# A decode step on one core: another plan of heads, and new orders of every engine's work

## The chip, the core and the metric

The kernel runs on one core of one Trainium2 chip. The core has five engines, each with its own instruction stream: TensorE (PE, with its weight loads shown as PEld), VectorE (DVE), ScalarE (ACT), GpSimd (POOL) and SyncE (SP), which here only issues transfers. The metric is the device time of one execution in microseconds (us): the median of the runs of a kernel. The span is the time from the first to the last instruction in the profile.

## The reference

Four sequences (B = 4), one new token each, model width 448. There are two layers with the same weights, each an attention block and an FFN block, with a layer norm ahead of each and a residual add behind:

```python
W = min(4096, max(256, Sk // 4))                  # 2048 of 8192 cached keys
q = (x @ wq).reshape(B, Sq, Hq, Dh)               # 16 query heads, 8 K/V heads, Dh = 256
k = jnp.repeat(k_cache[:, :, Sk - W:, :], rep, axis=1)
v = jnp.repeat(v_cache[:, :, Sk - W:, :], rep, axis=1)
scores = jnp.einsum("bhqd,bhkd->bhqk", q, k) * (Dh ** -0.5)
p = _softmax(scores, axis=-1)
o = jnp.einsum("bhqk,bhkd->bhqd", p, v)           # then o @ wo
x = x + _A_ref(_layernorm(x), ...)                # attention
x = x + _B_ref(_layernorm(x), ...)                # FFN: (silu(x @ w_gate) * (x @ w_up)) @ w_down
# ... and both once more
```

Each (sequence, K/V head) has a window of K and one of V, 1 MB each in bf16; 32 such pairs are needed in each layer. Both layers read the same 64 MB of cache. The weights are about 12 MB.

## The kernel before

**Heads and groups.** A head is named by three digits, sequence, layer and K/V head: 215 is sequence 2, layer 1, head 5. `PLAN` lists the heads in steps; a step's heads joined with `+` or `&` form one softmax group of two heads, and a group with `&` computes its scores head by head. A group runs through: scores (L878, PE), maximum (L894, DVE), two matmuls that spread it (L899, L902), its negative (L908), exp (L912, ACT), a turn of the probabilities (L925, PE) and their copy (L934, ACT), sums (L942, L947), P.V in two halves of a V matrix for each head (L956, PE), the pick of the right parts (L971 ACT, L973 DVE), a flip (L979, PE), the scaling into `oT` (L989, DVE) and the output projection, as rows (L1009) or, at a sequence's last step of a layer, as columns (L1001).

**Between layers.** When a sequence has all eight heads of a layer, its rows are folded in (L746, L748, L756), the residual is added (L764), and the norm runs (L519, L522 on DVE, L525 and L533 on PE, three small operations on POOL). Behind layer 0 follow its FFN, as columns (gate and up L705, down L733) for sequences 0 and 3 or as rows (L641, L669) for 1 and 2, and the projection of its queries for layer 1 (L579, L595, L610). Sequences that have ended layer 1 wait and share an FFN with a later one. The last FFN serves sequences 2 and 3 and ends the kernel.

**Memory.** K and V live in a pool of 27 slots of half a matrix (512 KB). `KEEP_K` and `KEEP_V` say how many heads of each sequence keep K or V from layer 0 to layer 1, so that they are loaded once. K has to be transposed by DVE in place, half by half (L845, 1232 ns each). The heads in `WHOLE` load K in one 1-MB transfer (L833), the others in two (L839); V always comes in two (L855). All transfers are issued by SyncE in one order. A load into a used slot waits for the last reader of what lay there, and whatever stands behind it in SyncE's order waits too.

**Orders.** `SEQ_PE`, `SEQ_DVE`, `SEQ_ACT`, `SEQ_POOL` and `SEQ_SP` list every operation of each engine in its order, by number; `SLOTS` gives each load its slot. An engine never runs ahead of its list. `w6` in `SEQ_PE` is a filler: a matmul of 128x512 on zeros into bank A (L1084) whose result adds nothing. It stands behind the 6th operation of another engine on bank A, and the 7th waits for it:

```python
if x[0] == "w":
    o, k = Op(len(self.ops), PE, "fw", filler), max(int(x[1:]), 1)
    o.deps[inA[max(k, 1) - 1]] = True
    if k < len(inA):
        inA[k].deps[o] = True
```

`DUR` holds a duration for each kind of operation. The order doesn't come from it: it only decides which waits are already covered by others and need not be written.

Of the kernel before, what the change touches and what calls it, by code (L numbers as in the profile page):

```python
# [35 lines left out]
KEEP_K = (6, 5, 4, 7)  # L36
KEEP_V = (5, 5, 4, 4)
ROWF = (1, 2)
PLAN = (
# [4 lines left out]
)  # L44
WHOLE = (
    "000 001 104 111 112 205 207 312 315 317"
)
SEQ_PE = (
# [32 lines left out]
)  # L81
SEQ_DVE = (
# [67 lines left out]
    guc1=.51, tanhc=.27, downc=1.65, rowcp=.54, rturn=.35, orow=.53, xin=.26, tr=1.24, qe=.29, sc1=.85, sc2=1.5, sch=1.2, max1=.25,  # L150
# [1000 lines left out]
```

## Time and profile before

| | |
|---|---|
| runs | 294.18, 295.67, 296.25 us; median 295.67 |
| profiled execution | 294.49 us, its span 292.6 us |
| mean granted TensorE clock | 0.953 |
| busy PE, PEld, DVE, ACT, POOL | 251.8, 137.6, 187.3, 63.2, 84.4 us |
| bytes loaded | 104.45 MB, mean 359 GB/s |
| fillers (L1084) | 294, 86.0 us busy |

A row of a time line gives the start, the length, the engine, the line and the operation, `out<-in` by the program's names, the shape and the count; in brackets stands idle time ahead of it and what ended it. `half` is the pool of K and V, `S`, `Y`, `Z` and `A` are banks of PSUM. SPq is SyncE's queue of DMA issues; a row that merges issues lasts from the first to the last of them, waits included. Matmuls overlap, so that their rows can be longer than what they add. A busy PE says little here, because fillers keep it busy while it waits.

### The profile page before, as it was taken

To read this page: it belongs to the slowest core of one execution; us is meant where nothing else is said; L and a number is where in the kernel's file an instruction comes from. 1 tells how busy PE (TensorE), PEld (TensorE's weight loads), DVE (VectorE), ACT (ScalarE), POOL (GpSimd) and SP (SyncE) were. 2 spreads that over 40 slices of the span, in tenths; PEclk is the share of its full clock that TensorE was granted. 3 is DMA by queue.
4 is the path that set the end of the run, shared out by engine and by line. 5 is a ranking of instruction groups with operands and counts; after the bars stand their busy time and mean duration, and the time that the engine had idled before them with its cause. 6 is when DMAs were issued, how large, how long until landed. Compare 5 with 4: busy or idle time off the path is not lost.

```text
span 292.6 us, 10922 instructions
## 1 busy us (share of the span) xinstructions
PE 251.8 (86%) x4814; PEld 137.6 (47%) x4814; DVE 187.3 (64%) x581; ACT 63.2 (22%) x176; POOL 84.4 (29%) x225
## 2 busy tenths in 40 slices
PE   0689889998999797988989978898798999799886
PEld 0334433334564463444435644544445447565554
DVE  8514985677114497658767969877596786336732
ACT  0030211212003121211333312313223221122310
POOL 1530231211304142403132453322444312244150
PEclk9999999999899797999999979999999995999959
DMA  7999999999999999989999999999999998599500
GB/s 266 401 392 407 410 410 407 408 408 404 391 407 325 381 393 406 408 317 313 413 405 395 417 414 407 407 409 409 403 374 410 409 398 270 212 330 399 230 4 3
DMA packets 29903, 105.15 MB, mean 359 GB/s; under 512 B 2968, under 2 KB 7072, under 8 KB 28448
## 3 DMA queue, kind: packets, MB, share of 16 engines
q1 hardware_dynamic: 29856, 104.45, 91.6%
q8 instruction: 38, 0.62, 0.9%
q14 instruction: 9, 0.07, 0.1%
HBM read 104.44 MB, written 0.00 MB: 357 GB/s over the span
## 4 chain that ended last, share of the span: by engine, by line
PE 44%; DMA 25%; DVE 18%; issue 5%; SPq 4%; ACT 2%; POOL 1%; DVEq 0%; ACTq 0%
DMA half<-in_A_k_cache_dram 15%; PE A L1084 11%; DMA half<-in_A_v_cache_dram 10%; DVE half L845 9%; PE Y L956 8%; PE S L878 8%; PE Z L705 3%; PE A L1009 2%; SPq L839 2%; DVE oh L973 2%; PE Z L733 2%; PE Z L525 2%; SPq L855 1%; DVE tiny L894 1%; PE S L899 1%
## 5 line engine op out<-in xcount | busy, mean ns | idle before, releaser
L845 DVE STREAM_TRANSPOSE half<-half 128x1024 uint32<-128x1024 uint32 x84 | 102.8, 1232 | 10.6 <-DMA half<-in_A_k_cache_dram 10.3
L1084 PE MATMUL A<-identb,small 128*128 128x512 bf16 x294 | 86.0, 394 | 0.7 <-ACT wide L746 0.5
L969 POOL TENSOR_TENSOR small<-small 128x2 f32<-128x2 f32 (+1 forms) x49 | 39.0, 797 | 67.2 <-DVE small L947 65.9
L956 PE MATMUL Y<-half,pT 128*4 128x256 bf16 (+1 forms) x1024 | 48.6, 283 | 9.2 <-issue 4.0
L878 PE MATMUL S<-half,qe 128*8 128x128 bf16 (+1 forms) x1568 | 46.0, 239 | 4.9 <-issue 2.6
L878 PEld LDWEIGHTS S<-half,qe 128*8 128x8 bf16 x1568 | 30.8, 85 | 17.0 <-DVE half L845 6.6
L884 POOL TENSOR_TENSOR qe<-qc,tiny 128x64 bf16<-128x64 bf16 x64 | 18.2, 293 | 70.6 <-PE S L878 57.6
L1084 PEld LDWEIGHTS A<-identb,small 128*128 128x128 bf16 x294 | 25.4, 101 | 20.0 <-issue 4.1
L912 ACT ACTIVATE praw<-S,small 104x128 bf16<-104x128 f32 (+1 forms) x49 | 19.6, 399 | 59.7 <-DVE small L908 59.5
L956 PEld LDWEIGHTS Y<-half,pT 128*4 128x4 bf16 (+1 forms) x1024 | 20.5, 85 | 23.7 <-DMA half<-in_A_v_cache_dram 8.4
L971 ACT ACTIVATE oh<-Y 128x256 bf16<-128x256 f32 x49 | 18.7, 383 | 53.1 <-PE Y L956 46.7
L973 DVE SCALAR_TENSOR_TENSOR oh<-oh,small,Y 128x256 bf16<-128x256 bf16 x49 | 23.1, 471 | 9.5 <-ACT oh L971 9.1
L894 DVE TENSOR_REDUCE tiny<-S 104x1 bf16<-104x128 f32 (+1 forms) x49 | 15.8, 324 | 17.6 <-PE S L878 17.0
L934 ACT ACTIVATE pT<-Y 128x64 bf16<-128x64 f32 (+1 forms) x49 | 12.5, 256 | 46.7 <-PE Y L956 26.3
L1009 PE MATMUL A<-wo_sb,oT 128*4 128x448 bf16 x188 | 17.3, 365 | 0.1
L541 POOL TENSOR_SCALAR st<-st 128x1 f32<-128x1 f32 x16 | 4.2, 265 | 34.5 <-DVE st L531 32.2
L947 DVE TENSOR_REDUCE small<-Y 128x2 f32<-128x32 f32 (+1 forms) x49 | 9.4, 192 | 7.4 <-PE Y L942 7.0
L525 PE MATMUL Z<-st,small 128*128 128x2 f32 x32 | 7.3, 299 | 7.5 <-DVE st L522 7.1
L989 DVE TENSOR_TENSOR oT<-Y,small 128x4 bf16<-128x4 f32 (+1 forms) x63 | 8.4, 151 | 7.7 <-PE Y L979 4.1
L899 PE MATMUL S<-small,identb 104*104 104x32 bf16 x49 | 10.6, 218 | 2.6 <-DVE tiny L894 1.7
L908 DVE TENSOR_REDUCE small<-S 104x1 f32<-104x32 f32 x49 | 8.7, 180 | 6.2 <-PE S L902 3.9
L899 PEld LDWEIGHTS S<-small,identb 104*104 104x104 bf16 x49 | 6.1, 126 | 11.9 <-DVE tiny L894 8.8
(132 smaller groups left out, 255.3 us busy)
## 6 DMA issues: line engine op xcount, KB each, us to landing
half<-in_A_v_cache_dram SPq DMA_DIRECT2D x92, 512.0 KB, 9.7
half<-in_A_k_cache_dram SPq DMA_DIRECT2D x68, 512.0 KB, 9.7
half<-in_A_k_cache_dram SPq DMA_DIRECT2D x8, 1024.0 KB, 9.7
wo_sb<-in_A_wo_dram SPq DMA_DIRECT2D x8, 448.0 KB, 11.4
wq_sb<-in_A_wq_dram SPq DMA_DIRECT2D x3, 1024.0 KB, 6.8
wd_sb<-in_B_w_down_dram SPq DMA_DIRECT2D x1, 1568.0 KB, 16.7
wg_sb<-in_B_w_gate_dram SPq DMA_DIRECT2D x1, 1344.0 KB, 13.1
wu_sb<-in_B_w_up_dram SPq DMA_DIRECT2D x1, 1344.0 KB, 15.2
```

Of the source, the lines that this page charges most:

```text
L845: return e.transpose(a, a)
L878: last = e.matmul(Sb[s_][qd:qd + 8, 0:32 * 2 * J], lhsT=qe[q_][:, P, ce, :, :].rearrange("p a n -> p (a n)"), rhs=keys(kcs[P], J * x, J, c ...
L884: g.op(POOL, "qe", lambda e, P=P, t=t, kvh=kvh: e.tensor_tensor(qe[q_][:, P, :, :, :], qc[t][:, kvh, :, :].unsqueeze(2).broadcast_to([128, ...
L894: g.op(DVE, f"max{n}", lambda e: e.tensor_reduce(pmax[s_][0:R, :], Sb[s_][0:R, 0:N], AX.X, ALU.max), r=(f"s{s_}",), w=(f"pmax{s_}",), bank ...
L899: e.matmul(Sb[s_][0:R, 256:288], lhsT=identb[0:R, 0:R], rhs=far[0:R, :, :, :].broadcast_to([R, 2, 8, 2]) if n == 2 else far1[0:R, :, :].br ...
L912: return e.activation(praw[0:R, 0:128 * n].rearrange("p (g r l) -> p g r l", g=2 * n, l=2), Sb[s_][0:R, 0:128 * n].rearrange("p (l g r) -> ...
L956: last = e.matmul(Yb[p_][32 * gg:32 * gg + M, 256:512], lhsT=pT[pt][:, gg, 2 * a + hv, 4 * P:4 * P + M] if n == 2 else p1[:, gg % 2, 2 * a ...
L969: g.op(POOL, f"pow{n}", lambda e: e.tensor_tensor(ri[p_][:, 0:2 * n], rs[p_][:, 0:2 * n], expo[:, 1:1 + 2 * n], op=ALU.pow), r=(f"rs{p_}", ...
L971: g.op(SCA, "oh", lambda e: e.activation(oh[:, :], Yb[p_][:, 256:512], ACT.Copy), r=(f"y{p_}",), w=("oh",), bank=(f"Y{p_}",))
L973: g.op(DVE, "oho", lambda e: e.scalar_tensor_tensor(out=oh[:, :], in0=oh[:, :], scalar=lomask[:, 0:1], in1=Yb[p_][:, 256:512], op0=ALU.mul ...
L1009: last = e.matmul(Ab[32 * k:32 * k + B, 0:D], lhsT=oT[oi][:, k % 2, k // 2, :], rhs=wo_sb[:, 4 * kvh + k, :], start=False, stop=False, ski ...
L1084: return e.matmul(Ab[:, 0:512], lhsT=zero[:, 0:1].broadcast_to([128, 128]), rhs=identb[:, :].unsqueeze(1).broadcast_to([128, 4, 128]), sta ...
```

## The change

Only tables change. `PLAN` has 50 groups (36 of one head, 14 of two) instead of 49 (34 and 15), in another order. 39 matrices are kept instead of 40: K 21 for 22, V 18 as before, but shared out otherwise. `WHOLE` names 18 heads instead of 10; of these, 15 instead of 8 are really loaded, since the others keep K from layer 0. So SyncE issues 182 transfers instead of 187. All five orders and the slots are new, the fillers are 344 instead of 294, and two durations in `DUR` differ. The text of the kernel is one line longer, so that from `SEQ_PE` on its line numbers are one higher.

```diff
-KEEP_K = (6, 5, 4, 7)
-KEEP_V = (5, 5, 4, 4)
+KEEP_K = (5, 5, 4, 7)
+KEEP_V = (6, 5, 4, 3)
 PLAN = (
-    "000 001", "004 006", "005", "002 003", "007", "101", "100", "102", "014", "013", "016&015", "017+107", "106",
-    "105", "104+103", "012 201+202 011", "204", "010 117+200", "114 113", "115&206", "203", "116", "207+205",
-    "112&111", "110", "302&303", "300 215", "213", "304+216", "307", "306", "301&217", "305", "212", "210",
-    "214 316+314", "311&315", "317+310", "313+211", "312",
+    "000", "002 005", "004", "007", "006", "001", "003", "102", "100", "101", "013", "016", "011+104",
+    "015+014 105", "017", "106+103", "107", "201 010", "200", "202", "012", "204&116", "110+203", "114", "115",
+    "207", "206", "113+205", "112+302", "117&306", "305", "111 213", "217+300", "307", "304+216", "303 301", "215",
+    "212", "210 214", "313+317", "311+314", "211", "312+315", "316&310",
 )
 WHOLE = (
-    "000 001 104 111 112 205 207 312 315 317"
+    "000 002 003 004 005 006 007 010 011 100 101 102 107 114 115 200 202 206"
 )
 SEQ_PE = (
-    "51 55 58 65 68 w1 75 w1 78 w1 85 w1 88 97 98 100 101 103 w1 w1 104 w1 106 w1 w1 w1 w1 w1 w1 w1 w1 w1 w1 w1 "
+    "w1 w1 w1 w1 w1 51 55 w1 w1 w1 58 w1 w1 65 w1 w1 w1 68 w1 w1 w1 w1 75 w1 w1 w1 w1 78 w1 w1 w1 85 w1 w1 97 w1 "
...
 SEQ_SP = (
-    "46 47 48 49 50 162 163 212 213 239 287 288 314 117 140 166 168 189 191 120 121 216 218 143 144 241 243 170 "
+    "50 46 47 142 48 49 117 120 190 121 214 164 238 146 264 193 145 262 139 242 287 361 167 217 168 186 212 236 "
...
-    guc1=.51, tanhc=.27, ... max1=.25,
+    guc1=.6, tanhc=.27, ... max1=.29,
```

The rows below are of the built programs, PE's instructions in their order, without times. `half` with `pT` is P.V, `half` with `qe` scores, `A<-identb,small` a filler, `wg_sb` and `wu_sb` gate and up, `wd_sb` down, `wo_sb` the output projection, `st,small` the norm's sums.

PE before, around the first row fold of sequence 1 (L756), while the V of heads 104 and 103 is used:

```order
L1084 MATMUL A<-identb,small 128x512 x2
L956 MATMUL Y<-half,pT 8x256 x8
L756 MATMUL Z<-tiny,wide 128x1 x8
L956 MATMUL Y<-half,pT 8x256 x8
L1084 MATMUL A<-identb,small 128x512 x13
L956 MATMUL Y<-half,pT 8x256 x8
L878 MATMUL S<-half,qe 8x256 x32
L956 MATMUL Y<-half,pT 8x256 x8
```

PE after, around the same fold (there L757):

```order
L1085 MATMUL A<-identb,small 128x512
L757 MATMUL Z<-tiny,wide 128x1 x8
L943 MATMUL Y<-pT,tiny 128x32
L980 MATMUL Y<-tiny,oh 128x2 x2
L1085 MATMUL A<-identb,small 128x512
L957 MATMUL Y<-half,pT 4x256 x8
L1085 MATMUL A<-identb,small 128x512
L926 MATMUL Y<-sel,praw 64x32 x4
L957 MATMUL Y<-half,pT 4x256 x8
```

Before, 13 fillers stand in a row between two P.V halves; after, fillers stand singly between the groups' operations.

PE before, in the FFN behind sequence 3's layer 0 (`wg_sb` to `wd_sb`):

```order
L956 MATMUL Y<-half,pT 4x256 x8
L533 MATMUL Z<-xn,twice 128x1
L705 MATMUL Z<-xn,wg_sb 128x32 x42
L705 MATMUL Z<-st,wg_sb 128x32 x14
L705 MATMUL Z<-xn,wu_sb 128x32 x42
L705 MATMUL Z<-st,wu_sb 128x32 x14
L979 MATMUL Y<-tiny,oh 128x2 x2
L1084 MATMUL A<-identb,small 128x512 x2
L733 MATMUL Z<-wide,wd_sb 128x32 x56
L1009 MATMUL A<-wo_sb,oT 4x448 x4
L925 MATMUL Y<-sel,praw 64x32 x4
L878 MATMUL S<-half,qe 8x128 x32
```

PE after, in the same FFN:

```order
L534 MATMUL Z<-xn,twice 128x1
L706 MATMUL Z<-xn,wg_sb 128x32 x42
L706 MATMUL Z<-st,wg_sb 128x32 x14
L926 MATMUL Y<-sel,praw 64x32 x4
L706 MATMUL Z<-xn,wu_sb 128x32 x42
L943 MATMUL Y<-pT,tiny 128x32
L706 MATMUL Z<-st,wu_sb 128x32 x14
L957 MATMUL Y<-half,pT 4x256 x16
L879 MATMUL S<-half,qe 8x128 x32
L926 MATMUL Y<-sel,praw 64x32 x4
L734 MATMUL Z<-wide,wd_sb 128x32 x56
```

The P.V of head 212 moved from ahead of gate and up to behind them, the scores of head 214 (the last row before) from behind the down matmuls to ahead of them, and the two fillers ahead of the down matmuls went.

PE before, from the last P.V to the last FFN:

```order
L956 MATMUL Y<-half,pT 4x256 x16
L533 MATMUL Z<-xn,twice 128x1
L756 MATMUL Z<-tiny,wide 128x1 x8
L1084 MATMUL A<-identb,small 128x512
L979 MATMUL Y<-tiny,oh 128x2 x2
L1084 MATMUL A<-identb,small 128x512
L1001 MATMUL A<-oT,wo_sb 128x1 x16
L1084 MATMUL A<-identb,small 128x512 x2
L525 MATMUL Z<-st,small 128x2
L1084 MATMUL A<-identb,small 128x512
L705 MATMUL Z<-xn,wg_sb 128x32 x42
```

PE after, the same stretch:

```order
L957 MATMUL Y<-half,pT 8x256 x32
L757 MATMUL Z<-tiny,wide 128x1 x8
L1085 MATMUL A<-identb,small 128x512
L980 MATMUL Y<-tiny,oh 128x4 x2
L1085 MATMUL A<-identb,small 128x512
L1002 MATMUL A<-oT,wo_sb 128x1 x32
L534 MATMUL Z<-xn,twice 128x1
L526 MATMUL Z<-st,small 128x2
L1085 MATMUL A<-identb,small 128x512
L534 MATMUL Z<-xn,twice 128x1
L706 MATMUL Z<-xn,wg_sb 128x32 x42
```

The last group now has two heads (316 and 310, before 312 alone), so that two column projections stand there, and the two fillers behind them went.

More of the change, by code (lines that the diff above doesn't have):

```diff
@@ L149 @@
     qturn=.25, qsel=.28, rvh=.24, rvt=.28, gur3=1.2, gur1=.7, tanhr=.69, fturn=.26, downr=.93, fh=.23, ft=.29, guc3=1.26,
-    guc1=.51, tanhc=.27, downc=1.65, rowcp=.54, rturn=.35, orow=.53, xin=.26, tr=1.24, qe=.29, sc1=.85, sc2=1.5, sch=1.2, max1=.25,
+    guc1=.6, tanhc=.27, downc=1.65, rowcp=.54, rturn=.35, orow=.53, xin=.26, tr=1.24, qe=.29, sc1=.85, sc2=1.5, sch=1.2, max1=.29,
     max2=.42, spread=.3, negm=.18, exp1=.36, exp2=.47, turn1=.26, turn2=.35, pt1=.22, pt2=.33, tot1=.19, tot2=.23,
```

165 rows, old and new, of tables (SEQ_ACT, SEQ_DVE, SEQ_PE, SEQ_POOL) are left out of this document.

## The prediction

> **What bounds the kernel now.** The page comes first: what it moves, and what the chain that ended last is made of.
>
> ```profile
> span 292.6 us, 10922 instructions
> PE 44%; DMA 25%; DVE 18%; issue 5%; SPq 4%; ACT 2%; POOL 1%; DVEq 0%; ACTq 0%
> q1 hardware_dynamic: 29856, 104.45, 91.6%
> ```
>
> The chain is PE's for 44% and a transfer's for 25%. These are averages over stages with different limits, so the second view is busy time by stretch, cut where the transfer rate changes (columns: PE, PEld, DVE, ACT, POOL busy; granted clock; DMA share; GB/s).
>
> ```profile
> 0.00:90.00 90.00, 74.73 (x1075) 35.81 (x1079) 49.62 (x179) 11.95 (x36) 19.96 (x58) 0.98 1.00 391
> 90.00:126.00 36.00, 30.74 (x637) 16.26 (x629) 24.02 (x60) 9.49 (x27) 11.46 (x28) 0.91 1.01 387
> 126.00:157.00 31.00, 27.98 (x541) 14.00 (x537) 21.95 (x61) 7.55 (x19) 8.41 (x25) 1.00 0.95 361
> 157.00:239.00 82.00, 71.90 (x1535) 41.00 (x1523) 64.80 (x179) 22.74 (x63) 28.64 (x74) 0.98 1.02 406
> 239.00:277.00 38.00, 34.52 (x821) 22.61 (x819) 21.85 (x76) 9.61 (x27) 11.93 (x30) 0.91 0.82 302
> 277.00:292.60 15.60, 11.96 (x250) 7.91 (x246) 5.01 (x30) 1.88 (x6) 3.99 (x11) 0.78 0.01 3
> ```
>
> Take 406 GB/s, the rate over the longest full stretch, as what the loads get when nothing holds them back. Each stretch then lost (1 - rate/406) of its length: 3.3, 1.7, 3.4, 0, and 9.7 us from 239 to 277. After that 15.6 us have no loads at all. So transfers set the pace up to 239 us. From there PE does, and the loads wait for it.
>
> The third view is the SyncE queue and PE around the two stretches that lose, first 126 to 157.
>
> ```profile
> half<-in_A_v_cache_dram SPq DMA_DIRECT2D x1, 512.0 KB, 15.3
> 111.18 5.59 SPq L855 DMA_DIRECT2D half<-in_A_v_cache_dram  x2
> 116.82 13.84 SPq L839 DMA_DIRECT2D half<-in_A_k_cache_dram  x4
> 126.07 2.98 PE L1084 MATMUL A<-identb,small 128*128 128x512 bf16 x13
> 128.98 0.39 PE L956 MATMUL Y<-half,pT 128*8 128x256 bf16 x8
> 129.20 1.09 PE L878 MATMUL S<-half,qe 128*8 128x256 bf16 x32
> ```
>
> The first row is the DMA view of 111 to 112 us: that half of V landed 15.3 us after its issue at 111.18, at 126.5. The P.V matmuls on it (L956) began at 128.98, because 13 fillers stood ahead of them. The scores behind (L878) ended at 130.3, and the queue, which needed their slot, had nothing issued before that. Without the run the P.V starts at about 126.5: 2.5 us.
>
> From 239 on, PE's time line reads so:
>
> ```profile
> 237.75 0.39 PE L956 MATMUL Y<-half,pT 128*4 128x256 bf16 x8
> 242.31 1.07 PE L878 MATMUL S<-half,qe 128*8 128x128 bf16 x32
> 247.08 0.60 PE L705 MATMUL Z<-st,wu_sb 128*128 128x32 bf16 x14
> 248.45 1.56 PE L733 MATMUL Z<-wide,wd_sb 128*128 128x32 bf16 x56
> 253.20 0.82 PE L579 MATMUL Z<-wq_sb,xn 128*4 128x512 bf16 x12
> 258.53 2.05 PE L878 MATMUL S<-half,qe 128*8 128x256 bf16 x48
> 278.30 0.61 PE L956 MATMUL Y<-half,pT 128*4 128x256 bf16 x16
> 280.41 0.59 PE L1001 MATMUL A<-oT,wo_sb 128*128 128x1 bf16 x16
> 280.86 1.01 PE L1084 MATMUL A<-identb,small 128*128 128x512 bf16 x2
> 282.54 0.59 PE L525 MATMUL Z<-st,small 128*128 128x2 f32 x2 [0.66 <-DVE st L522]
> ```
>
> At 237.75 the last P.V of sequence 3's layer 0 runs. Its FFN and q projection follow, strictly in PE's order, and only at 258.53 do the first scores of sequence 3's layer 1 start: 20.8 us. Five groups follow, to the last P.V, which ends at 278.9: 20.4 us. The tail to 292.6 is 13.7. The sum is 54.85.
>
> **The change part by part.** *Bytes.* One head matrix fewer is kept: 105.49 MB instead of 104.44, +1.05 MB, or 2.6 us at 406 GB/s if the loads decide the end. If PE's chain after 237.75 decides it, another count matters. By the SyncE order and the sizes on the page, the half of V that ends sequence 3's layer 0 is now the load with which 90.80 MB are in; before it was 91.85. That stretch begins 1.05 MB earlier: **-2.6**. In exchange 14.69 MB instead of 12.59 come behind it.
>
> *1-MB transfers.* Fifteen loads of K instead of eight go in one transfer. The rows give no price to that: 157 to 239 holds both sizes at 406 GB/s, the sizes' common limit, so **0**. What covers it is the queue of issued loads. [...]
>
> *The filler run.* The order now puts single fillers between the operations there: **-2.5**. The row next to it bounds it: between 0 (the queue then waits for the next group) and 3.4, all that the stretch lost.
>
> *Early work.* Fillers go from 294 to 344, and 43 of the 50 added ones stand where the first 30 MB are still coming in and transfers set the pace. By 2.98/13 = 0.23 us each they are 10 us of PE time, hidden behind the queue: by the new order 17 MB are issued before the first load that waits for a slot. **0**. If that cover were gone, it would be up to those 10. Reordered set-up on DVE and K ahead of V at the start are hidden by the same loads.
>
> *Sequence 3's FFN.* Between the marks 237.75 and 258.53 the new order has the same FFN and projection, and in addition the scores of one head (L878, 0.63 us, the price just ahead of the mark, quoted below), a pair of P.V halves (0.61, as at 278.30), a column projection (0.59, as at 280.41), a row projection (0.4, taken like a P.V half) and two fillers (0.23 each): 2.7 us.
>
> ```profile
> 237.29 0.63 PE L878 MATMUL S<-half,qe 128*8 128x128 bf16 x32
> ```
>
> Lower end 0 (PE waited there anyway), upper end 5.4, twice as much, if the transposes it needs come late. I take **+2.7**, since PE is busy 3.8 to 4.0 of 4 us in that stretch (rows below).
>
> *Five last groups.* The same five (four of two heads, one of one), with 1 filler instead of 9: 8 x 0.23 = **-1.8**, between 0 and -3.
>
> *Tail.* The residual add waited for two fillers behind the projection:
>
> ```profile
> 281.91 0.16 DVE L764 TENSOR_TENSOR xr<-xr,A 128x4 f32<-128x4 f32 x1 [1.56 <-PE A L1084]
> ```
>
> The projection ended at 281.0, the add began at 281.9. That 0.9 goes, and a second column projection comes in (L1001, at most 0.59, taken as 0.4 since PE overlaps them): **-0.5**. What is then late is the norm's chain on DVE.
>
> *The rest.* One more softmax group adds small operations to stretches in which PE has work for 74.7 of 90 or 71.9 of 82 us, and the two new numbers in the table of durations change which waits are written out, not the order: **0**.
>
> **Sum**, on the profiled execution: 292.6 - 2.6 - 2.5 + 2.7 - 1.8 - 0.5 = **287.9 us span**. That execution took 294.49, 1.9 over its span, and the median of the runs shown is 295.67, another 1.2: 287.9 + 3.1 = **291.0**, 1.6% less. A difference of 1% (3.0 us) is about what a measurement of this kernel can tell from no change.
>
> **The rivals.** *The loads decide.* If PE keeps ahead, the 14.69 MB after the mark take 36.2 us at 406 GB/s. The mark stands at 237.75 - 5.1 = 232.7, so they end at 268.9, and with a P.V (0.6) and a tail of 13.2 the span is 282.7, the time 285.8. For it: the transposes of the last K now come earlier. Against it: the rate was 302 in this stretch.
>
> *A cold clock.* Where the clock was down, PE was not idle:
>
> ```profile
> 240.00:244.00 4.00, 3.77 (x70) 2.32 (x71) 2.59 (x11) 0.00 (x0) 0.76 (x2) 0.69 0.76 284
> 244.00:248.00 4.00, 4.00 (x126) 3.50 (x119) 2.49 (x8) 0.93 (x3) 1.66 (x5) 0.50 0.90 280
> ```
>
> The same score group took 1.07 us at 242.31, against 0.63 before. Of about 6.5 us below full clock, 41% is lost: 2.7 us. With 1 filler instead of 9 among the last groups such a stretch could fall there: span 290.6, time 293.7. [...]
>
> *The queue runs dry earlier, and it is slower.* The FFN of sequence 2 lies at 190 to 210. The DMA views of 178 to 184 us (first two rows) and of 209 to 214 (last two) show what it ate of the queue's stock:
>
> ```profile
> half<-in_A_v_cache_dram SPq DMA_DIRECT2D x3, 512.0 KB, 13.8
> half<-in_A_k_cache_dram SPq DMA_DIRECT2D x3, 512.0 KB, 13.4
> half<-in_A_k_cache_dram SPq DMA_DIRECT2D x3, 512.0 KB, 8.1
> half<-in_A_v_cache_dram SPq DMA_DIRECT2D x3, 512.0 KB, 7.3
> ```
>
> From issue to landing it fell from 13.6 to 7.7: 5.9 us of stock used, no load held up. Counted through the new order, the loads freed during this FFN stand only 2.1 to 3.2 MB (5 to 8 us) behind the one that their releaser needs; before it was 2.6 to 5.2. If the stock is gone when the FFN starts, these 5.9 us are lost, and with the same at sequence 1 the 2.5 aren't won: 287.9 + 8.4 = 296.3, time 299.4, slower by 1.3%. It decides once the loads lose over 8 us between 126 and 239. Against it: PE has 10 us without work in the 82 of that stretch.
>
> *The gains are given back.* The FFN of sequence 3 costs its upper end (+2.7), and the filler run another wait (+2.5): 293.1, time 296.2, no change.
>
> **How the numbers follow.** Forecast 0.50, the loads decide 0.12, cold clock 0.12, dry queue 0.14, given back 0.12. The forecast's own range is 288.5 to 293.5 by the ends of its small terms; a sixth of it lies above 292.7, where 1% begins. Faster: 0.42 + 0.12 = 0.54. Within 1%: 0.08 + 0.12 of the clock, 0.04 of the dry queue (half its price), 0.08 of the last = 0.32. Slower: 0.10 + 0.04 = 0.14. The range, 285.0 to 298.5, takes in all but most of the dry queue and some of each end.
>
> **What would show it.** In the profile after: no run of over ten fillers ahead of a P.V at about 125 us, and 126 to 157 near 390 GB/s. The mark (last P.V of sequence 3's layer 0) at about 233; the first scores of its layer 1 some 23.5 us later; the last P.V 18.6 after that; a tail near 13.2. The prediction is wrong if the rate between 157 and 230 falls under 390 (the dry queue), or if the last groups' P.V wait for transfers rather than for PE's own order.

## The result, and the profile after

Changed kernel: 287.2 us (median of 4, 285.39 to 291.14), beside 295.89 (4 runs, 294.18 to 296.25); the ratio is 0.970 (0.963 to 0.976). Run once more (e1 below) it gave 288.7 beside 295.35, 0.980 (0.969 to 0.990). Forecast were 291.0 and 1.6% less; it is 2 to 3% less. 287.2 lies inside the whole range (285.0 to 298.5), but below the forecast's own (288.5 to 293.5). Executions over 1.5% above the quickest of their kernel are left out of the ratios and of all medians below, and as both traced executions of the changed kernel (291.1 and 292.9 us) are such, run e3, the same orders in an execution of 288.3, stands beside them where lengths are compared. By that the changed kernel's median over both runs is 287.2 (6 executions).

The page of the changed kernel, the same three lines as before:

```profile
span 289.4 us, 11132 instructions
PE 41%; DMA 37%; DVE 14%; SPq 3%; ACT 2%; issue 2%; POOL 0%; DVEq 0%
q1 hardware_dynamic: 29136, 105.50, 93.6%
```

"issue" went from 5% of the chain to 2%. Busy time by stretch, columns as before (PE, PEld, DVE, ACT, POOL busy; granted clock; DMA share; GB/s):

```profile
0.00:90.00 90.00, 77.14 (x1111) 39.03 (x1111) 48.14 (x178) 11.80 (x36) 18.05 (x55) 1.00 1.00 394
90.00:126.00 36.00, 32.68 (x677) 16.74 (x677) 27.76 (x61) 9.20 (x27) 11.59 (x30) 1.00 1.01 391
126.00:157.00 31.00, 27.45 (x520) 14.32 (x516) 23.90 (x71) 8.55 (x23) 9.74 (x30) 0.94 1.00 389
157.00:239.00 82.00, 70.32 (x1523) 39.42 (x1522) 61.63 (x172) 22.08 (x61) 26.94 (x74) 0.99 1.00 394
239.00:277.00 38.00, 34.70 (x872) 23.27 (x870) 23.32 (x85) 11.26 (x31) 13.47 (x36) 0.93 0.88 324
277.00:289.40 12.40, 8.27 (x222) 6.51 (x222) 3.68 (x24) 0.79 (x3) 3.16 (x10) 0.82 0.01 3
```

From 126 to 157 the loads go from 361 to 389 GB/s, from 239 to 277 from 302 to 324. Then the marks on PE's time line, and the residual add on DVE's:

```profile
235.62 0.39 PE L957 MATMUL Y<-half,pT 128*4 128x256 bf16 x8 [1.48 <-DMA half<-in_A_v_cache_dram]
258.99 2.03 PE L879 MATMUL S<-half,qe 128*8 128x256 bf16 x64 [0.63 <-POOL qe L885]
275.52 1.29 PE L957 MATMUL Y<-half,pT 128*8 128x256 bf16 x32
278.28 0.95 PE L1002 MATMUL A<-oT,wo_sb 128*128 128x1 bf16 x32
```

```profile
279.27 0.16 DVE L765 TENSOR_TENSOR xr<-xr,A 128x4 f32<-128x4 f32 x1 [0.71 <-PE Z L534]
```

The mark (last P.V of sequence 3's layer 0) is at 235.6, 23.4 us later the first layer-1 scores of sequence 3 start, 17.8 later the last P.V ends (276.8), and the tail is 12.55. In e3:

```profile
232.85 0.39 PE L958 MATMUL Y<-half,pT 128*4 128x256 bf16 x8
255.13 1.12 PE L880 MATMUL S<-half,qe 128*8 128x256 bf16 x32 [0.63 <-POOL qe L886]
273.14 0.39 PE L958 MATMUL Y<-half,pT 128*8 128x256 bf16 x8 [0.59 <-DMA half<-in_A_v_cache_dram]
```

So 232.9, then 22.3, 18.4 and a tail of 12.6 (span 286.1). (A variant's line numbers are off by a few.) From the mark to the last P.V it takes 41.2 us before, and 41.2 and 40.7 after. What was won lies ahead of the mark and in the tail.

### The profile page after: what moved, and what is told of

Read it like the earlier page. It is cut to its first block, busy times and chain, and to the rows that moved or that the text cites. A ratio compares the mean times of both kernels' runs of the same rounds, so it can differ in the third digit from the quotient of the medians.

```text
span 289.4 us, 11132 instructions
## 1 busy us (share of the span) xinstructions
PE 250.6 (87%) x4912; PEld 139.3 (48%) x4912; DVE 188.4 (65%) x587; ACT 63.7 (22%) x179; POOL 82.9 (29%) x234
## 4 chain that ended last, share of the span: by engine, by line
PE 41%; DMA 37%; DVE 14%; SPq 3%; ACT 2%; issue 2%; POOL 0%; DVEq 0%
DMA half<-in_A_k_cache_dram 22%; DMA half<-in_A_v_cache_dram 15%; PE A L1085 11%; PE S L879 8%; DVE half L846 8%; PE Y L957 6%; PE Z L706 3%; PE A L1010 2%; PE Y L926 2%; PE Z L734 2%; PE A L1002 1%; DVE oh L974 1%; SPq L834 1%; PE Z L580 1%; SPq L492 1%
## 5 line engine op out<-in xcount | busy, mean ns | idle before, releaser
L846 DVE STREAM_TRANSPOSE half<-half 128x1024 uint32<-128x1024 uint32 x86 | 105.2, 1233 | 12.6 <-DMA half<-in_A_k_cache_dram 12.5
L1085 PE MATMUL A<-identb,small 128*128 128x512 bf16 x344 | 102.4, 395 | 5.2 <-DVE A L420 4.8
L957 PE MATMUL Y<-half,pT 128*4 128x256 bf16 (+1 forms) x1024 | 44.7, 275 | 7.5 <-DMA half<-in_A_v_cache_dram 4.7
L879 PE MATMUL S<-half,qe 128*8 128x128 bf16 (+1 forms) x1600 | 42.6, 238 | 6.1 <-POOL qe L885 2.1
L1085 PEld LDWEIGHTS A<-identb,small 128*128 128x128 bf16 x344 | 29.4, 103 | 31.9 <-issue 9.6
L879 PEld LDWEIGHTS S<-half,qe 128*8 128x8 bf16 x1600 | 29.5, 85 | 18.0 <-POOL qe L885 4.1
L957 PEld LDWEIGHTS Y<-half,pT 128*4 128x4 bf16 (+1 forms) x1024 | 19.0, 83 | 20.4 <-DMA half<-in_A_v_cache_dram 6.7
L935 ACT ACTIVATE pT<-Y 128x64 bf16<-128x64 f32 (+1 forms) x50 | 12.6, 251 | 36.0 <-PE Y L926 31.5
L1037 POOL MEMSET oT<- 128x16 bf16 x40 | 4.1, 111 | 36.8 <-PE A L1010 24.1
L926 PE MATMUL Y<-sel,praw 104*64 104x32 bf16 x144 | 8.8, 193 | 4.0 <-ACT praw L913 3.6
L980 PEld LDWEIGHTS Y<-tiny,oh 128*128 128x128 bf16 x100 | 6.9, 100 | 10.7 <-DVE oh L974 5.4
```

The source lines that it names most:

```text
L846: return e.transpose(a, a)
L879: last = e.matmul(Sb[s_][qd:qd + 8, 0:32 * 2 * J], lhsT=qe[q_][:, P, ce, :, :].rearrange("p a n -> p (a n)"), rhs=keys(kcs[P], J * x, J, c ...
L926: last = e.matmul(Yb[p_][64 * h:64 * h + 64, c0:c0 + (48 if n == 2 else 32)], lhsT=praw[0:R, 64 * gg:64 * gg + 64], rhs=w, start=(gg == 0) ...
L957: last = e.matmul(Yb[p_][32 * gg:32 * gg + M, 256:512], lhsT=pT[pt][:, gg, 2 * a + hv, 4 * P:4 * P + M] if n == 2 else p1[:, gg % 2, 2 * a ...
L1085: return e.matmul(Ab[:, 0:512], lhsT=zero[:, 0:1].broadcast_to([128, 128]), rhs=identb[:, :].unsqueeze(1).broadcast_to([128, 4, 128]), sta ...
```

## The experiments

In the table all lengths are read from PE's time line of the one traced execution; "issue" is the sum of PE's idle pieces of 0.35 us and more, from 90 us on, that the trace puts down to nothing but issue.

```
run                     median (n)   beside  ratio (95%)            mark  to scores  to last P.V  tail   issue
before                  -            -       -                     237.8     20.8         20.4  13.7     6.6
e2  before, no run      292.7 (9)    293.8   0.996 (0.991-1.000)   234.6     18.2         22.8  13.7     6.6
e5  before, end         294.7 (9)    294.9   0.999 (0.994-1.003)   238.6     21.2         20.2  12.9     6.8
e9  before, less bytes  294.6 (9)    293.6   1.006 (1.002-1.010)   236.4     20.9         20.1  13.6     7.0
after                   286.7 (3)    295.9   0.970 (0.963-0.976)   235.6     23.4         17.8  12.6     0.0
e1  after again         288.0 (3)    293.8   0.980 (0.969-0.990)   235.7     23.3         19.6  12.6     0.0
e3  after, split        287.4 (2)    293.8   0.978 (0.968-0.989)   232.9     22.3         18.4  12.6     0.0
e4  after, 43 fewer     287.1 (1)    293.8   -                     230.4     21.5         20.8  12.6     2.1
e6  after, less ahead   287.0 (5)    294.9   0.971 (0.966-0.976)   230.8     23.6         18.3  12.6     2.3
e7  after, less behind  286.1 (5)    294.9   0.969 (0.964-0.974)   229.5     21.9         18.1  12.6     0.7
e8  after, no FFN fill  286.1 (3)    294.9   0.969 (0.963-0.976)   233.0     21.4         20.9  12.9     0.0
e10 after, none early   290.7 (9)    293.6   0.990 (0.987-0.994)   230.6     26.4         20.8  12.6     5.0
e11 after, P.V ahead    286.8 (5)    293.6   0.979 (0.973-0.986)   231.6     21.6         18.9  12.6     0.0
e12 e11 and e8          286.3 (4)    293.6   0.977 (0.971-0.982)   233.3     21.7         21.2  12.6     0.0
```

### e1: the change again

No edit.

> The changed kernel once more, unaltered, for a second trace. Its first traced execution took 291.14 us; its three others took 285.4 to 287.7. In that first trace sequence 3's layer 0 ends (last P.V) at 235.6 us, first layer-1 scores of sequence 3 at 259.0 (23.4 later), the last P.V ends at 276.8 (17.8 later), the tail is 12.6, and the loads ran at 379 GB/s from 190 to 215 us. Theory A (the PE order from that P.V on is a fixed chain of 23.4 + 17.8 + 12.6 us, and only the loads ahead of it vary): a trace with a time near 287 has the P.V at about 231.5, the same three lengths within 0.7 us, and 190 to 215 near 400 GB/s. Rival B (the last stretches vary): the P.V stays at about 235 and the lengths behind it are 4 us shorter.

The trace took 292.9, and its mark was at 235.7 again, so theory A was not put to the test as meant. The later traces do that: executions of 283.8 to 288.3 (e3, e4, e6, e7, e11) have the mark at 229.5 to 232.9. The length from the mark to the last P.V is not fixed, but moves only between 40.7 and 42.9 in the traces that keep the orders and the bytes behind the mark (after, e1, e3, e4, e6), with one exception: 47.2 in e10.

### e2: the run of 13 fillers alone

```diff
-... 603 615 604 w6 w6 w6 w6 w6 w6 w6 w6 w6 w6 w6 w6 w6 605 703 606 705 ...
+... 603 615 604 605 703 606 705 ...
```

> The kernel before without the 13 fillers that stand ahead of the P.V at 128.98 us; nothing else is changed. Forecast's step: 2.5 us sooner, so the last P.V of sequence 3's layer 0 starts at about 235.2 instead of 237.75, 126 to 157 us runs at about 390 GB/s instead of 361, and the time is about 293.2. Rival (the queue then waits for the next group): 361 rises by less than 10, time 295.7, no change.

The stretch 126 to 157 and the marks of e2:

```profile
126.00:157.00 31.00, 29.21 (x584) 15.18 (x576) 22.95 (x66) 8.76 (x23) 9.19 (x27) 0.94 1.01 391
```

```profile
234.55 0.39 PE L956 MATMUL Y<-half,pT 128*4 128x256 bf16 x8
252.77 1.42 PE L878 MATMUL S<-half,qe 128*8 128x256 bf16 x38
275.01 0.61 PE L956 MATMUL Y<-half,pT 128*4 128x256 bf16 x16
```

391 GB/s instead of 361, as forecast; the other two traces of the order before, e5 and e9, have 369 and 355 there. The mark came 3.2 sooner, in one trace beside one. The median is 1.2 lower, with an interval from 0 to 2.6. The place is right; of the size the times say no more than that.

### e5: the fillers of the end alone

```diff
-... 1516 1496 w28 1541 ... 1501 1519 w28 1521 1544 w28 1505 ... 1631 w33 1627 w33 1633 w33 w33 1637 ...
+... 1516 1496 1541 ... 1501 1519 1521 1544 1505 ... 1631 w33 1627 w33 1633 1637 ...
```

> The kernel before, with 8 of the 9 fillers among its five last groups taken out, and the two that stand behind its last column projection. Forecast's steps: from the first layer-1 scores of sequence 3 to the end of the last P.V 18.6 us instead of 20.4, and the tail behind it shorter by the 0.9 that the residual add waited, 12.8 instead of 13.7; the time 2.7 lower than the kernel before beside it. Rival (cold clock): the granted clock over the last groups, 1.00 in the trace of before, falls to about 0.9 and the stretch stays at 20 us. Rival (loads): the last load landed at 276.4 and its P.V can't end ahead of about 277, so of 1.8 at most that much comes; the P.V then waits for a transfer.

```profile
238.60 0.39 PE L955 MATMUL Y<-half,pT 128*4 128x256 bf16 x8
259.77 1.96 PE L877 MATMUL S<-half,qe 128*8 128x256 bf16 x48
279.36 0.61 PE L955 MATMUL Y<-half,pT 128*4 128x256 bf16 x16
```

```profile
282.08 0.16 DVE L763 TENSOR_TENSOR xr<-xr,A 128x4 f32<-128x4 f32 x1 [0.69 <-PE A L1000]
```

Two answers in one trace. The tail fell from 13.71 to 12.87, the 0.9 that the add had waited; now it waits for the projection (L1000). The five groups took 20.2 instead of 20.4: taking eight fillers out of them gave nothing, and the clock there stayed at 1.00, so the cold clock was not what ate it. Nor were the loads: the last one landed at 278.7, 1.3 ahead of the end of the last P.V, and no wait of PE in the five groups is put down to a load. PE's waits there, of 0.15 us and more and all put down to DVE and ACT, went from 0.7 to 2.7 us: where the fillers ran, PE now waits for the groups' own small operations. The tail's gain does not show in the median (0.2 of 294.9, with an interval of -1.8 to 1.0).

### e3: 1-MB transfers split

```diff
-                        g.dma(1 << 20, lambda e, kc=kc, ksrc=ksrc: e.dma_start(
-                            kv[:, HALF * kc[0][0]:HALF * kc[0][0] + 2 * HALF], ksrc[:, :]), None, ...
+                        g.dma(1 << 20, lambda e, kc=kc, ksrc=ksrc: tuple(e.dma_start(
+                            kv[:, HALF * (kc[0][0] + b):HALF * (kc[0][0] + b + 1)], ksrc[:, HALF * b:HALF * (b + 1)])
+                            for b in range(2)), None, ...
```

> The changed kernel with each of its 15 transfers of 1 MB issued as two of 512 KB, one behind the other, on the same place in the queue, into the same slots and behind the same waits. Forecast's step (the size of a transfer is worth 0): 287.2 within 1 us. Rival (1-MB transfers move faster: the first 29 us brought 11.1 MB after and 10.6 before, 1.3 us at 406 GB/s): 288.5 to 289.5, with the loss ahead of 90 us, where 14 of the 15 are. A third, that the smaller pieces land sooner and help: 286.

Its four runs (286.4 to 292.8) don't tell 0 from the rival's 1.3 us. In the trace PE's operations between 75 and 135 us come up to 1.3 us later than in the changed kernel's first trace, and from 155 on level or sooner; beside e6, which has the same orders and the 1-MB transfers, they come 2 to 3 us later from 40 to 97 us. The first 29 us brought 362 GB/s in e3 (366 or 367 in the traces of the order before) and 373 to 389 in the nine other traces of the new orders: 0.3 to 0.8 MB, which is 0.8 to 1.9 us at 406 GB/s. That speaks for the rival, in the place that it names, though e3 has one trace; what it is worth at the end stays open.

### e6 and e9: fewer bytes ahead of the mark

```diff
+                        if (t, layer, kvh) in ((3, 0, 0), (3, 0, 7)):
+                            g.dma(1 << 18, lambda e, cell=cell, hv=hv, vsrc=vsrc: e.dma_start(
+                                unit(cell)[:, 0:HALF // 2], vsrc[hv][:, 0:HALF // 2]), None, ...
```

e6 has this in the changed kernel, e9 in the kernel before, there for heads 2 and 3.

> The changed kernel with 1.05 MB less to load ahead of the end of sequence 3's layer 0: the four V halves of its heads 0 and 7 bring 256 KB each instead of 512 (the second half of each is left out of the computation; the same number of transfers, slots and waits). Forecast's step (the mark moves with the bytes ahead of it, 2.6 us per 1.05 MB at 406 GB/s): last P.V of layer 0 of sequence 3 about 2.6 sooner against the bytes' pace, the loads' queue no longer in the way, and the time 284.5 to 285.5. Rival (PE's order ahead of the mark decides it): time 287 to 288, no change.

> The kernel before with 1.05 MB less to load ahead of the end of sequence 3's layer 0: the four V halves of its heads 2 and 3 bring 256 KB each (their second half is left out of the computation). They land at 201 to 207 us in the trace of before, where a load had 11 to 13 us from issue to landing. Forecast's step (in the kernel before, bytes ahead of the mark set it): the last P.V of sequence 3's layer 0 at about 235.2 instead of 237.75 (238.6 in the other undisturbed trace), time 292.5 beside 295. Rival (as in the changed kernel, where the same cut gave nothing: the issue of the next loads waits for PE's FFN of sequence 2, and the stock is only used up sooner): the mark within 0.8 us of before, the rate from 200 to 230 us under 385, time 294.5 to 295.

The stretch 200 to 230, first e3 and e6, then the kernel before and e9, each from its own windows:

```profile
200.00:230.00 30.00, 26.07 (x638) 15.58 (x639) 23.44 (x71) 8.99 (x24) 9.47 (x29) 1.00 1.02 403
```

```profile
200.00:230.00 30.00, 26.10 (x596) 15.02 (x585) 21.87 (x68) 9.17 (x26) 10.52 (x34) 0.94 0.97 354
```

```profile
200.00:230.00 30.00, 25.79 (x591) 14.61 (x583) 22.18 (x70) 8.89 (x24) 11.27 (x32) 1.00 1.01 400
```

```profile
200.00:230.00 30.00, 26.50 (x628) 15.57 (x626) 22.38 (x71) 9.17 (x25) 11.07 (x32) 1.00 0.99 385
```

In e6 the rate fell by 49 GB/s over 30 us, which is 1.5 MB, and the DMA share from 1.02 to 0.97: the loads behind did not use the room. Each is issued only when its slot is free, and what SyncE waited for between 196 and 226 us was in every case a matmul of PE. The half of V that the mark's P.V reads was issued at 220.74 in e6 and took 10.0 us; in e4 and e7, with all the bytes ahead of the mark, it was issued at 219.94. The time is that of the changed kernel. In e9 the mark of the one trace came 1.4 sooner, but its runs were 0.6% slower than before, not 0.9% faster. A megabyte ahead of the mark is not worth 2.6 us in either kernel. That step of the forecast fell.

### e7: fewer bytes behind the mark

The same edit for heads 0 and 4 of sequence 2's layer 1.

> The changed kernel with 1.05 MB less to load behind that mark: the four V halves of heads 0 and 4 of sequence 2's layer 1 bring 256 KB each (their second half is left out of the computation). Forecast's step (behind the mark PE's chain decides, the number of bytes there doesn't): time within 0.7 us of the changed kernel, the last load lands about 2 us sooner and the last P.V does not. Rival (the loads decide the end): 2 to 2.6 us sooner, with the last P.V moving together with the last load. By the traces so far it lies between: in two of them the last P.V ended 0.7 to 1.0 us behind the last landing, in another 2.9 behind.

286.1, 1.1 under the changed kernel's 287.2, and 0.9 under e6, whose bytes were cut to no use; neither is clear of the spread. Mark to last P.V took 40.0, and the last P.V ended 0.75 behind the last landing (268.7). The number of bytes behind the mark is worth less than the rival's 2 to 2.6, and may be worth nothing.

### e8, e11 and e12: the stretch behind the mark

e8 takes out the 12 fillers there, e11 moves two P.V halves (1417, 1418) ahead, e12 does both:

```diff
-... 1342 1415 1343 w27 1351 w27 1347 w27 1417 1353 w27 1354 1418 1211 1433 w28 w28 1422 ...
+... 1342 1415 1417 1418 1343 1351 1347 1353 1354 1211 1433 1422 ...
```

> The changed kernel without the 12 fillers that stand between the last P.V of sequence 3's layer 0 and the first layer-1 scores of sequence 3. Forecast's price for a filler on the path (0.23 us): 2.8 us sooner; the chain of waits of the first trace has 3.55 us of fillers in that stretch (at a granted clock of 0.85). Rival (PE waits there for transposes and norms anyway): the stretch stays at 21.4 (clock 1.00) to 23.4 (clock 0.85), time unchanged. Rival (cold clock): granted clock there under 0.8 and the stretch 24 or more, time 1 to 2 us later.

> The changed kernel with the two P.V halves of head 5 of sequence 2 moved ahead of the last P.V of sequence 3's layer 0, which waits for its load; in the order of the change they stand behind it and each releases a load. Theory (behind the mark the loads decide as much as PE, and what they lose is the 5 to 7 us in which nothing is issued there): the next load is issued at about 2 us ahead of the mark's P.V instead of 2 behind it, the last load lands 1 to 2 us sooner against the mark, and mark to last P.V takes 39.5 to 40.5 us instead of 41.2 to 42.9; time 286 to 287. Rival (PE's chain decides): 41 to 42 as before, no change of the time.

> The same, and without the 12 fillers between the mark and the first layer-1 scores of sequence 3. Theory (loads decide, and the fillers hold back the P.V and scores that release slots): another 0.5 to 1.5 us off mark to last P.V, 38.5 to 40. Rival (the fillers keep the clock up and cost nothing): granted clock under 0.85 in that stretch, mark to last P.V as in the run without the fillers alone, 42.

No version is faster than the changed kernel. e11 took 40.5 from mark to last P.V, which theory and e3 (40.7) both give. Without the fillers the clock fell, in e8 (first fence) and e12 (second):

```profile
236.40:239.80 3.40, 2.04 (x49) 1.50 (x43) 3.40 (x12) 0.39 (x1) 0.26 (x2) 0.61 1.00 393
239.80:243.20 3.40, 3.40 (x99) 2.75 (x96) 1.96 (x7) 0.64 (x2) 2.38 (x8) 0.50 0.99 381
```

```profile
232.20:235.60 3.40, 2.05 (x51) 1.28 (x50) 1.83 (x5) 0.77 (x2) 1.36 (x2) 1.00 1.01 406
235.60:245.80 10.20, 8.30 (x223) 6.95 (x227) 8.39 (x27) 1.29 (x5) 3.30 (x12) 0.50 0.91 335
245.80:249.20 3.40, 2.91 (x111) 2.60 (x99) 1.62 (x13) 0.86 (x3) 0.20 (x1) 0.99 0.66 219
```

In e12 a window in which PE was busy 2.05 of 3.4 us is followed by 10.2 us at 0.50: 5.1 us of PE's work lost for 12 fillers saved. In these two traces half clock cost PE 5.1 and 8.5 us between 230 and 272, in after, e1, e3, e4, e6 and e11 0 to 3.4. In the executions behind the medians the mean granted clock was 0.966 or 0.967 in e8, beside 0.973 to 0.992 in the changed kernel; in e12 (0.975 to 0.981) it was no lower than in e11 (0.972 to 0.984), so for e12 the loss is not shown beyond its trace. The three medians lie 0.4 to 1.1 us under 287.2: by the times the fillers there are worth about nothing either way.

### e4 and e10: the early fillers

e4 takes out 43 of the 174 that wait only for the set-up, e10 all:

```diff
-w1 w1 w1 w1 w1 51 55 w1 w1 w1 58 w1 w1 65 w1 w1 w1 68 w1 w1 w1 w1 75 w1 ...
+51 55 58 65 68 75 ...
```

> The changed kernel with 43 of the 174 fillers of the first stretch (those that wait for nothing but the set-up) taken out, evenly spread: as many as the change added there. Forecast's step (they lie under the loads): 287.2 within 1 us, and the bytes that have come in by 90 us the same within 0.3 MB. Rival (the clock gate needs them): the granted clock ahead of 90 us falls under 0.95 and the time rises by 1 to 3 us. Rival the other way (they cost PE time on the path): 1 to 3 us sooner.

> The changed kernel without any of the 174 fillers of the first stretch. Forecast's step (they lie under the loads): time within 1 us of the changed kernel (287 to 288 over its runs), the same MB in by 90 us. Rival (cold clock: PE without them is idle for long, the granted clock ahead of 60 us falls to about half): PE's groups there are late, the loads behind the first slots wait for them, and the time is 2 to 5 us longer. The trace with 43 fewer spoke for the forecast (PE's operations 1 to 2 us sooner), three timed executions of it (291.9 to 293.4) against it.

The first 90 us of e10:

```profile
0.00:29.00 29.00, 10.41 (x138) 5.90 (x138) 16.35 (x91) 2.55 (x3) 7.35 (x29) 0.89 0.95 389
29.00:60.00 31.00, 17.75 (x352) 11.54 (x356) 20.18 (x46) 5.08 (x18) 5.42 (x11) 0.50 1.03 405
60.00:90.00 30.00, 24.31 (x481) 14.79 (x469) 11.96 (x45) 4.59 (x16) 6.46 (x18) 0.77 1.03 398
```

The clock went to half for 50 us, and nothing was late by it: the same loads, and the mark at 230.6, among the soonest. By that the fillers there are worth 0, as forecast. Yet e10's median is 3.5 us above the changed kernel's 287.2, and 4 above those of e11 and e12, measured beside it. (e4 has one execution that counts, the traced one, at 287.1: no difference.) In e10's trace the loss is in another place: from the mark to the last P.V it takes 47.2 us, where after, e1, e3, e4 and e6 take 40.7 to 42.9. PE's time line of e10, then of e4:

```profile
246.06 0.22 PE L874 MATMUL S<-half,qe 128*8 128x128 bf16 x2 [2.24 <-issue]
266.53 0.71 PE L952 MATMUL Y<-half,pT 128*8 128x256 bf16 x17 [1.73 <-issue]
```

```profile
261.41 0.72 PE L956 MATMUL Y<-half,pT 128*8 128x256 bf16 x20 [1.28 <-issue]
```

PE stands still in the middle of a group of matmuls, some 200 us behind the place of the edit, for 4.0 us in these two pieces of e10, and 6.8 and 3.4 us at half clock begin 1.6 us behind each. The kernel before has the same:

```profile
98.00 0.69 PE L878 MATMUL S<-half,qe 128*8 128x256 bf16 x5 [1.48 <-issue]
111.95 0.38 PE L956 MATMUL Y<-half,pT 128*8 128x256 bf16 x1 [1.86 <-issue]
170.20 0.38 PE L956 MATMUL Y<-half,pT 128*4 128x256 bf16 x4 [1.48 <-issue]
226.50 0.28 PE L956 MATMUL Y<-half,pT 128*4 128x256 bf16 x4 [0.63 <-issue]
252.10 0.28 PE L878 MATMUL S<-half,qe 128*8 128x128 bf16 x7 [1.14 <-issue]
```

6.6 us in five pieces, and in e2, e5 and e9, which nearly keep its order, 6.6 to 7.0, at least four of the pieces at the same instructions. In the changed kernel's two traces no piece put down to issue is left. In the groups of instructions the costliest idle of these two lines reads, before and after (page, last column):

```profile
L956 PE MATMUL Y<-half,pT 128*4 128x256 bf16 (+1 forms) x1024 | 48.6, 283 | 9.2 <-issue 4.0
L878 PE MATMUL S<-half,qe 128*8 128x128 bf16 (+1 forms) x1568 | 46.0, 239 | 4.9 <-issue 2.6
```

```profile
L957 PE MATMUL Y<-half,pT 128*4 128x256 bf16 (+1 forms) x1024 | 44.7, 275 | 7.5 <-DMA half<-in_A_v_cache_dram 4.7
L879 PE MATMUL S<-half,qe 128*8 128x128 bf16 (+1 forms) x1600 | 42.6, 238 | 6.1 <-POOL qe L885 2.1
```

What the pieces have in common comes out by counting PE's instructions (weight loads, matmuls, waits) in the trace: all 31 of them, in the eight traces of the table that have any, begin at number 194 + 256 n, give or take one. The page of before has a queue of instructions with 38 packets and 0.62 MB, 16 KB each; PE has 9,674 instructions, which is one packet per 256:

```profile
q8 instruction: 38, 0.62, 0.9%
```

The five blocks of before, by the same count:

```
block ends at    block begun   used in    PE idle   goes on at
instr. 2498         91.9         4.3        1.5        98.0
instr. 3010        106.2         3.6        1.9       111.9
instr. 5058        164.6         4.0        1.5       170.2
instr. 7106        220.1         5.5        0.6       226.5
instr. 8130        246.6         4.2        1.1       252.1
```

By the trace's record of these packets, in before one starts 0.2 to 4 us behind the instant at which PE enters a block while there are loads, and 1.4 and 0.0 us behind the last two, when they are over; that the loads hold it up is the author's reading of these figures, and no run tests it. It takes about 1.0 us (0.9 to 1.1 ahead of the five waits), and PE went on about 1.4 us behind its end. Ahead of the five waits the packet started 3.1 to 3.8 us behind, so PE went on 5.5 to 6.4 us behind its entry, however soon it was done. Two more blocks of before, used up in 4.1 and 4.6 us (from 209.4 and 241.9), end without a wait: their packets started 1.6 and 1.1 us behind. Scores use instructions up fastest (64 in 0.63 us), fillers most slowly (2 in 0.23): a filler more or fewer anywhere moves all block ends behind it. The new order is not free of dense blocks: at instruction 8130 (249.2 us) a P.V stands for 0.96 us, which the profile puts down to a DVE operation whose result it doesn't read; in e1 and e3 it is 1.55 and 1.12 us, and in e6 the same place shows 1.84 us of issue.

## Why the prediction came out, step by step

The way came out, and the number lies inside the range, but the sum did not give it. 4.7 us were forecast and 6 to 9 measured, one term of 2.6 gave nothing, and gains that the sum does not have made up for it. That the total came as near as it did is in part luck.

**The filler run (-2.5)**: right in place (391 GB/s, 3.2 us at the mark of one trace); by the times 1.2, between 0 and 2.6.

**The bytes (-2.6)**: this is the step that failed. It took the 406 GB/s from 157 to 239 as proof that transfers set the pace, and so priced a megabyte. e6 and e9 took a megabyte away and got nothing in the median. The mark does wait for a load: its P.V starts within 0.05 us of the landing of its half of V in after, e1, e2, e3, e5, e6, e7 and e8. But when that load lands hangs on when PE frees its slot, some 10 us ahead, and fewer bytes did not bring that forward.

**Sequence 3's FFN (+2.7)**: right, if a little low. 23.4 against 20.8 with 6.8 us at half clock in each (+2.6); at full clock it is 18.2 in e2 against 21.5 and 22.3 in e4 and e3.

**Five last groups (-1.8)**: the size came out (17.8 and 18.4 for 20.4), the reason in part at most: eight fillers fewer gave 0.2 in e5, where 2.0 us more of waits for DVE and ACT took their place. In the new order all of PE's waits there are 0.5 us (after) and 1.7 (e3). The two stretches behind the mark are one: 41.2 together, before and after. What the first takes on, the second no longer has; how much of that is PE's and how much the loads' the runs don't part.

**The tail (-0.5)**: undersized, -1.15 (13.71 to 12.55). The two fillers gave 0.85 in e5 alone, as forecast (0.9); the second column projection, priced at 0.4, cost nothing.

**Early fillers and transfer size (0)**: nothing is late ahead of the mark without the fillers, so the price is right where it was looked for. It left out that they also set where the 256-instruction blocks end. The size of the transfers was priced from 157 to 239, but 14 of the 15 large ones come ahead of 90 us, and there the traces show 0.8 to 1.9 us; whether they reach the end is open.

**What the sum lacks.** By the tested steps the change is worth 1.2 to 3.2 (run) and 1.15 (tail), with mark to last P.V at par: 2 to 4 of the 6 to 9 us that the two ratios give. Two things in the record could make up the rest. One was in view: "issue" 5% on the first line quoted from the chain, with PE's 6.6 us of waiting for instructions in it. The traces of the new order (after, e1, e3) have none of it under that name, and 1.0 to 1.6 us at instruction 8130. No run isolates what this is worth. e10 fits it: 174 fillers taken out from under the loads, 5.0 us of these waits back, and a time 3.5 us above the changed kernel's 287.2. Against it: e4 has 2.1 us and e6 2.3 us of such waits, and neither is slower (287.1, one execution, and 287.0), and e10 has one trace. The other is the 1-MB transfers at the start, see e3. So the larger part of the gain stays open.

**The rivals.** The loads deciding the end (285.8) comes nearest in time. As a mechanism it is not borne out: P.V waits for loads in the last groups, which the prediction named as a sign against itself, take 0 us in after, 0.9 in e1, 0.6 in e3 and 0.4 in e4, and e7 leaves about 1 us to it. The dry queue: from 157 to 230 us the rate was 393 GB/s in after and 405 in e3, not under the 390 that was named as its sign. The cold clock among the last groups: 1.00 in after and e3, 3.4 us at half in e4. (The piece of before from which it was priced is 6.83 us at 0.50, which loses 3.4 us, not 2.7.) The gains given back: the FFN took 2.6 to 4.1 us more, not 5.4.

## What to carry to other kernels

Idle time that a profile gives to "issue" in the middle of a group of matmuls is worth a term of its own: count the instructions, and see whether the pieces lie a fixed number apart. Where PE runs short instructions in bursts, try to spread them so that no block of 256 is used up in much under 6 us while loads queue; the 6 us is an estimate from this case, where the blocks that waited were used up in 3.6 to 6.0 us. And a rate at its ceiling does not show that bytes are the bound: see what the issue of each load waits for, and take some bytes away before pricing them.

## What the runs showed of the hardware

- The 31 places in which PE stood still, for 0.5 to 2.4 us each, lie 256 instructions apart in their trace, or a multiple of it, give or take one. PE's 9,674 instructions by the 38 packets of 16 KB on the page of before are 255 to a packet. PE had used up the 256 ahead in 3.6 to 6.0 us while loads queued, and the packet for the next had started 2.3 to 4.4 us behind its entry. Every trace of the old order has such places, 6.6 to 7.0 us of them in all.
- In these traces half clock came in pieces of 3.4 us or whole multiples of it: 3.4 (before, 98.2 to 101.6), 6.8 (after, 237.2 to 244.0) or 10.2 long (e12), in e10 once 51.2. Read in windows of 0.4 us around the first three waits above, the clock of before is 0.50 or 1.00, and something else (0.55 to 0.98) only in a window in which it changes. Such a piece began within 0.4 us of the end of each of these three waits; the kernel before, inside the pieces:

```profile
98.20:101.40 3.20, 3.20 (x42) 1.66 (x37) 2.66 (x4) 0.22 (x1) 1.29 (x3) 0.50 1.02 413
112.00:115.20 3.20, 3.20 (x28) 1.30 (x28) 2.61 (x6) 0.42 (x3) 0.22 (x2) 0.50 1.03 417
170.00:173.20 3.20, 3.00 (x49) 1.42 (x48) 2.09 (x4) 0.38 (x1) 1.42 (x4) 0.50 1.03 422
```

  There 3.4 us at 0.50 took another 1.7 of PE's work beside a wait of 1.5 to 1.9 us; in e9 the waits of 1.2 and 2.4 us at 97 and 110 us were followed by none. The prediction's row of 244 to 248 us, 0.50 granted to a PE that was busy 4.00 of 4.00, lies in a piece of before that came behind a stretch in which PE had idled: 2.82 of 3.4 us busy from 238.1 to 241.5, then half clock to 248.3. Whether the idling brought it on is not shown, nor why it lasted a second 3.4 us: PE was busy 3.17 of the first 3.4.
- From 90 to 126 us the loads ran at 387 GB/s in before and at 404 in e9, whose program is the same up to there, at DMA shares of 1.01 and 1.02. No run says why.
